# Two small rows, D and the shift weights, moved from ScalarE's DMA queue to the head of SyncE's

## The chip, the cores and the metric

The kernel runs on one NeuronCore of a Trainium2 chip. The metric is the device time of one execution in microseconds; a median of several runs is given with its lowest and highest. The engines are TensorE (PE, with its weight loads as PEld), VectorE (DVE), ScalarE (ACT), GpSimd (POOL) and SyncE (SP). SyncE and ScalarE can issue DMA transfers; the issuing instructions stand in the profile as SPq and ACTq.

## The reference

Two independent parts are computed, and their outputs stand side by side in one array of 2048 x 1152 in bf16. All inputs are bf16; S is 2048 and D is 576.

Part A is a long convolution per channel. With `kv = (k shifted and weighted by 4 taps) * v`:

```
k_shift = sum over t of k_pad[:, t:t + S, :] * shift_k[:, 3 - t]
kv      = k_shift * v
y       = irfft(rfft(kv padded to 2S) * rfft(ssm_k padded to 2S))[:S]   # along S, per channel
out_A   = q * (y + kv * ssm_D)
```

Part B is linear attention with 32 heads of 18 channels:

```
q, k, v = split(x @ wqkv);  phi(t) = where(t > 0, t + 1, exp(t)) + 1e-6
kv = einsum(phi(k), v);  z = sum over s of phi(k)
out_B = (einsum(phi(q), kv) / (einsum(phi(q), z) + 1e-6)) @ wo
```

## The kernel before

Part A is a transform of length 4096 made of matmuls. The 576 channels are cut into five chunks (`ACH`: four of 128, one of 64). A chunk of the filter (`h_sb`) is loaded with channels on partitions, transposed on TensorE into `hT`, and goes through a first stage (`h1`: matmuls with the matrices `G`, evicted into `Ch`), a transpose by DMA (`ht`, from `Ch` to `Cth`) and a second stage (`h2`). The signal kv goes the same way (`u1`, `ut`, `u2`). Products of the two, an inverse in two stages (`i1`, `i2`) and the multiplication by q follow. The term `kv * ssm_D` costs no pass of its own: D is added to the filter's first tap. The matrices `G` are made on the chip: VectorE computes indices (`ix`, tiles `mp` and `mc`), and ScalarE takes sines of them (`sin`). The second stage's small matrices come from GpSimd's indices (`iv`) and another sine (`sw`), after which ScalarE changes its table to the exponential.

Part B loads x in four groups of 512 rows (`x_sb`), transposes them on TensorE into `xT` (`x_D`; evicted by VectorE for groups 2 and 0), multiplies by the weights `wqk` for k and q, forms phi with an exponential on ScalarE and a multiply-max on VectorE, and then the head sums and the output matmuls.

The order of the work is written out by hand. `ORDER` is a string of some 300 units such as `ls` or `hT.0.D/21`; each unit's name stands for a function, the parts after dots are its arguments, and the digits after the slash choose buffers (PSUM places and rings). Every engine and every queue executes its share of the units in this order, and a waiting instruction holds up what stands behind it on its engine.

The head of the order, before: `io` (index rows by GpSimd, and the first sine on ScalarE, which loads its table); `ls` (load_shift, line 371: VectorE sets ones, ScalarE's queue loads the 4608-byte row of shift weights to one partition); `wu.0` (VectorE zeroes an operand); `ix.0.0`; `wu.1.A` (warm-up: five matmuls of zeros, line 81); `dl` (load_D, line 416: two memsets by VectorE, then ScalarE's queue loads the 1152-byte row of D); `id`, `iw` (identity and small indices); `sin.1.0`; `dc` (turn_D, line 422: five matmuls of one column turn the row of D into a column, which ScalarE copies to `Dcol`); `ix.0.1`; then the first chunks on SyncE's queue, `hl.0` (filter chunk 0), `xl.2` (x group 2), `hl.1` (filter chunk 1); `hd.0` (h_D, line 492: ScalarE adds D to the first tap of chunk 0); `Wj.A` (shift_w, line 376: matmuls with a column of ones spread the shift row to 128 partitions, ScalarE evicts them in three pieces); `hT.0.D` (line 498: 16 transposes of chunk 0, VectorE evicts); `sin.1.1`; `xl.0`; `xd.2` (16 and 4 transposes of x group 2, VectorE evicts both); `hd.1`; `sin.0.0` and `sin.0.1`; `hT.1`; and the first stages `h1`.

On SyncE's queue, the transfers follow one another so: filter chunk 0, x group 2, filter chunk 1, x group 0, three pieces of `wqk` with three pieces of k between the second and the third, and then the first transpose `ht.0.0`.

```
zero = K.sm[:, 1984:2048].bitcast(BF)
...
for _ in range({'A': 5, 'B': 8, 'C': 11, 'D': 14}[n]):
    nc.tensor.matmul(ps[:], lhsT=zero, rhs=zero.unsqueeze(1).to_broadcast([128, 4, 128]), start=True, stop=True)
```

Of the kernel before, what the change touches and what calls it, by code (L numbers as in the profile page):

```python
# [17 lines left out]
D = 576  # L18
# [11 lines left out]


ORDER = """
io ls wu.0 ix.0.0/0 wu.1.A/0 dl id iw sin.1.0 dc/1 ix.0.1 hl.0/0 xl.2 hl.1/1 ix.1.0/1 hd.0 ix.1.1 Wj.A/230 hT.0.D/21
sin.1.1 xl.0 xd.2.DD/023 hd.1 sin.0.0 sin.0.1 lw.2 hT.1.D/00 h1.0.0.1.A/01 h1.0.0.0.D/2 lw.1 h1.0.1.0.A/3 wm kl.0
h1.0.1.1.A/0 h1.1.1.0.A/11 iv lw.0 sw wk xd.0.DD/123 k.10/0 k.8/1 k.11/2 W k.2/3 ht.0.0/0 h1.1.0.0.A/0 cv.0.0.D k.0/1
k.1/2 hc h1.1.0.1.A/3 cv.0.1.DP k.3/0 q.2.1/1 k.9/2 h1.1.1.1.A/3 vl.0/0 cv.0.2.DD qt.0/0 xl.3 h2.0.0.1.A/01
# [37 lines left out]
def _warm(tc, psum, K, n):  # L74

    nc = tc.nc
    zero = K.sm[:, 1984:2048].bitcast(BF)
    if n:
        ps = psum.tile([128, 4, 128], FP32, name="warm_ps")
        for _ in range({'A': 5, 'B': 8, 'C': 11, 'D': 14}[n]):  # L80
            nc.tensor.matmul(ps[:], lhsT=zero, rhs=zero.unsqueeze(1).to_broadcast([128, 4, 128]), start=True, stop=True)
    else:
        nc.vector.memset(zero, 0.0)
# [162 lines left out]
def kernel(  # L246
# [13 lines left out]
    nc = tc.nc  # L260
# [87 lines left out]
    K = Consts()  # L348
# [17 lines left out]
    Wj = lpool.tile([128, 4, D], BF, name="Wj")  # L366
# [4 lines left out]
    def load_shift():  # L371
        K.Srow = pqT[0:1].rearrange("o c n -> o (c n)")[:, 0:4 * D]
        nc.vector.memset(K.sm[0:1, 769:833].bitcast(BF), 1.0)
        nc.scalar.dma_start(out=K.Srow, in_=A_shift_k.rearrange("(o d) j -> o (d j)", o=1))

    def shift_w(eng='A'):
        one = K.sm[0:1, 769:833].bitcast(BF)
# [38 lines left out]
    def load_D():  # L416
        K.Drow = K.sm[0:1, 448:769].bitcast(BF)
        nc.vector.memset(K.Drow[:, 576:640], 0.0)
        nc.vector.memset(K.Drow[:, 640:641], 1.0)
        nc.scalar.dma_start(out=K.Drow[:, 0:576], in_=A_ssm_D.rearrange("(o d) -> o d", o=1))  # L420

    def turn_D():
        K.D = ab.tile([128, 5], FP32, name="Dcol")
# [189 lines left out]
    B = {}  # L613
# [195 lines left out]
    def store_A(i):  # L809
# [5 lines left out]

    UNITS = {
        'xl': load_x, 'wm': one_w, 'lw': load_w, 'ls': load_shift, 'Wj': shift_w, 'eps': eps_col,
        'dl': load_D, 'dc': turn_D, 'id': lambda: _ident(tc, cpool, K), 'io': lambda: _small(tc, cpool, slotx, K),
        'ix': lambda p, h: _dft_index(tc, slotx, K, p, h), 'iv': lambda: _w16_phase(tc, K),
        'iw': lambda: _w16_index(tc, K), 'wk': lambda: _w16_mask(tc, K), 'sin': lambda ri, h: _sine(tc, cpool, K, ri, h),  # L820
# [17 lines left out]
        'i1': i1, 'i2': i2, 'st': store_A,  # L838
        'k': b_k, 'q': b_q, 'qt': b_qt, 'lwv': load_wv, 'wom': wo_M, 'lwo': load_wo, 'G': b_G, 'zs': b_z, 'kv': b_kv, 'M': b_M,
        'den': b_den, 'wu': lambda *n: _warm(tc, psum, K, n[-1]), 'bc': b_bc, 'bt': b_bt, 'o': b_out, 'ol': b_last,  # L840
    }
    with tc.manual_schedule():
        for unit in ORDER.split():
            unit, _, places = unit.partition("/")
# [33 lines left out]
```

## Time and profile before

| | |
|---|---|
| median of 3 runs (lowest to highest) | 164.46 us (163.96 to 164.61) |
| the profiled execution's own time | 162.77 us |
| its span, first to last instruction | 161.0 us |
| TensorE matmuls busy | 148.7 us (92%) |
| VectorE busy | 139.0 us (86%) |
| ScalarE busy | 127.3 us (79%) |
| GpSimd busy | 66.2 us (41%) |
| SyncE's DMA queue, packets' time | 89.2% of 16 engines' span |
| ScalarE's DMA queue | 4 packets, 0.01 MB |
| granted TensorE clock, mean | 0.999 |

Times in the profile are microseconds from the first instruction. A row of the timeline has the start, the duration, the engine, the line of the kernel, the operation, the tile written and the tiles read, and in brackets the engine's idle time before it with what ended that. Matmuls are pipelined and their ends are modelled. The chain of waits goes back from the last instruction to what released it, step by step, and is printed in order of time; a row has start, duration and name. A list of waits names the waiting instruction, what it waited for, the total, how often and the longest. The table of stretches gives for each stretch its length and, for each engine, busy time and number of instructions, then the granted clock, the share of the DMA engines' time and the GB/s. A DMA row's last number is the time from issue to landing.

### The profile page before, as it was taken

Reading aid. Unit: us, or ns where it says so; the run is one execution under the profiler, and the core shown is the slowest. Engines: PE = TensorE matmul, PEld = TensorE weight load, DVE = VectorE, ACT = ScalarE, POOL = GpSimd, SP = SyncE. Lnnn points to the kernel's source line nnn. Section 1 sums busy time; section 2 is a strip of 40 time slices with the busy share of each in tenths; the row PEclk is TensorE's granted clock in tenths of the full one; section 3 lists DMA queues with packets and bytes.
Section 4 is the critical chain, followed back from the end, with each engine's and each line's share of the span. In section 5 each row is a group of like instructions: output and inputs, shape, how many; then the busy total and the mean of one; then the engine's idle time right before and its main releaser. Section 6 shows DMA issues by size and latency. Waiting matters only on the chain.

```text
span 161.0 us, 4590 instructions
## 1 busy us (share of the span) xinstructions
PE 148.7 (92%) x1980; PEld 92.6 (58%) x1998; DVE 139.0 (86%) x171; ACT 127.3 (79%) x154; POOL 66.2 (41%) x68
## 2 busy tenths in 40 slices
PE   5699999999999999999999996999888999999982
PEld 1298555555643466657557476587545566578641
DVE  7969499699999898997999997998999989899631
ACT  5598786997998999998999674899987957596312
POOL 3007741806511819109000049199999068320000
PEclk9999999999999999999999999999999999999999
DMA  4999999592939699979999996698599995435175
GB/s 150 390 276 291 204 264 275 167 156 105 175 85 196 179 141 308 220 149 316 177 219 262 229 198 143 120 216 193 157 241 181 317 210 130 122 93 150 44 220 195
DMA packets 73084, 31.65 MB, mean 197 GB/s; under 512 B 50988, under 2 KB 72423, under 8 KB 73064
## 3 DMA queue, kind: packets, MB, share of 16 engines
q1 hardware_dynamic: 73060, 31.35, 89.2%
q8 instruction: 15, 0.25, 0.6%
q14 instruction: 5, 0.04, 0.1%
q10 hardware_dynamic: 4, 0.01, 0.0%
HBM read 14.97 MB, written 4.72 MB: 122 GB/s over the span
## 4 chain that ended last, share of the span: by engine, by line
PE 59%; DVE 14%; ACT 11%; DMA 7%; POOL 2%; issue 2%; SPq 1%; DVEq 0%; ACTq 0%
PE q_ps L456 11%; PE k_ps L447 9%; PE o_ps L773 8%; PE s_ps L551 5%; PE s_ps L528 5%; DMA wv_GT<-in_B_wqkv_dram 5%; PE i_ps L585 4%; DVE pqT L743 4%; ACT Cu L301 3%; ACT V L301 3%; PE g_ps L656 2%; DMA sm<-in_A_ssm_D_dram 2%; DVE at L486 2%; PE i_ps L598 2%; PE hT_ps L507 2%
## 5 line engine op out<-in xcount | busy, mean ns | idle before, releaser
L447 PE MATMUL k_ps<-wqk,xT 128*128 128x512 bf16 (+1 forms) x154 | 21.4, 282 | 0.4
L301 ACT ACTIVATE Ch<-s_ps 128x1024 bf16<-128x1024 f32 (+1 forms) x18 | 16.4, 953 | 3.9 <-PE s_ps L528 3.8
L528 PEld LDWEIGHTS <-G 128*128 128x128 bf16 x320 | 17.6, 98 | 3.0 <-issue 1.9
L456 PE MATMUL q_ps<-xT,wqk 128*128 128x512 bf16 x77 | 18.3, 379 | 0.2
L301 ACT ACTIVATE V<-i_ps 128x1024 bf16<-128x1024 f32 x17 | 16.6, 1039 | 1.3 <-PE i_ps L585 1.0
L447 PEld LDWEIGHTS <-xT 128*128 128x128 bf16 x160 | 11.4, 98 | 10.9 <-issue 0.9
L656 PE MATMUL g_ps<-pk,x_sb 128*128 128x65 bf16 (+1 forms) x124 | 16.3, 283 | 0.2
L301 ACT ACTIVATE T<-s_ps 128x1024 bf16<-128x1024 f32 x16 | 15.7, 1022 | 0.8 <-PE s_ps L551 0.8
L301 ACT ACTIVATE ob<-o_ps 128x576 bf16<-128x576 f32 (+1 forms) x11 | 6.8, 630 | 11.7 <-PE o_ps L765 7.8
L301 ACT ACTIVATE Cu<-s_ps 128x1024 bf16<-128x1024 f32 (+1 forms) x17 | 15.9, 984 | 0.0
L486 DVE TENSOR_TENSOR at<-at 128x2048 bf16<-128x2048 bf16 (+1 forms) x13 | 14.9, 1143 | 0.5
L485 DVE TENSOR_TENSOR at<-k,Wj 128x2048 bf16<-128x2048 bf16 (+1 forms) x13 | 14.8, 1136 | 0.4 <-POOL at L486 0.4
L301 ACT ACTIVATE SU<-s_ps 128x1024 bf16<-128x1024 f32 x14 | 14.1, 1044 | 0.6 <-PE s_ps L551 0.6
L773 PE MATMUL o_ps<-wo_M,pqT 128*128 128x64 bf16 (+1 forms) x107 | 14.1, 282 | 0.5 <-issue 0.3
L563 POOL TENSOR_TENSOR X<-SU,T 128x2048 bf16<-128x2048 bf16 x3 | 12.4, 4130 | 4.1 <-DMA Cth<-Ch 4.1
L483 POOL TENSOR_TENSOR at<-k,Wj 128x2048 bf16<-128x2048 bf16 (+1 forms) x2 | 6.2, 3094 | 19.1 <-PE s_ps L551 18.5
L440 DVE SCALAR_TENSOR_TENSOR pk<-pk,k_ps 128x576 bf16<-128x576 bf16 x16 | 11.8, 750 | 2.4 <-ACT pk L439 2.4
L656 PEld LDWEIGHTS <-x_sb 128*128 128x128 bf16 x128 | 8.5, 97 | 8.5 <-issue 0.8
L439 ACT ACTIVATE pk<-k_ps,neg 128x576 bf16<-128x576 f32 x16 | 11.6, 743 | 1.4 <-PE k_ps L447 1.0
L456 PEld LDWEIGHTS <-wqk 128*128 128x128 bf16 x80 | 7.4, 98 | 8.7 <-issue 0.9
L600 DVE TENSOR_TENSOR q<-i_ps,q 128x1024 bf16<-128x1024 f32 (+1 forms) x10 | 11.0, 1113 | 0.9 <-PE i_ps L599 0.9
L773 PEld LDWEIGHTS <-pqT 128*128 128x128 bf16 x112 | 7.5, 98 | 7.3 <-issue 0.7
(160 smaller groups left out, 346.2 us busy)
## 6 DMA issues: line engine op xcount, KB each, us to landing
x_sb<-in_B_x_dram SPq DMA_DIRECT2D x4, 576.0 KB, 6.4
h_sb<-in_A_ssm_k_dram SPq DMA_DIRECT2D x4, 512.0 KB, 4.3
out_dram<-ob SPq DMA_DIRECT2D x7, 288.0 KB, 2.7
k<-in_A_k_dram SPq DMA_DIRECT2D x1, 1280.0 KB
v<-in_A_v_dram SPq DMA_DIRECT2D x1, 1280.0 KB
q<-in_A_q_dram SPq DMA_DIRECT2D x1, 1280.0 KB, 8.7
wqk<-in_B_wqkv_dram SPq DMA_DIRECT2D x2, 576.0 KB
k<-in_A_k_dram SPq DMA_DIRECT2D x1, 1024.0 KB
```

The source lines that it names most:

```text
L301: nc.scalar.activation(out=out, in_=in_, func=ACT.Copy)
L439: nc.scalar.activation(out=out_ap, in_=ps_ap, func=ACT.Exp, bias=K.neg1[0:n, :])
L440: nc.vector.scalar_tensor_tensor(out=out_ap, in0=out_ap, scalar=1.0, in1=ps_ap, op0=ALU.min, op1=ALU.max)
L447: nc.tensor.matmul(ps[:, n0:n1], lhsT=xT[r // 4][:, t, rr * 128:(rr + 1) * 128], rhs=wqk[:, t, D + n0:D + n1], start=(t == 0), stop=(t == 4))
L456: nc.tensor.matmul(ps[:, j, :], lhsT=wqk[:, t, 128 * c:128 * c + 128], rhs=xT[g][:, t, :], start=(t == 0), stop=(t == 4))
L485: on[0].tensor_tensor(out=t_, in0=kk[:, 3 - stage:19 - stage], in1=wb(stage), op=ALU.mult)
L486: on[1].tensor_tensor(out=a_, in0=a_, in1=t_, op=ALU.add)
L528: nc.tensor.matmul(ps[:, bi, 0:dc], lhsT=K.G[ri][:, b, :], rhs=xf(b), start=True, stop=True)
L563: e.tensor_tensor(out=s['X', hf][:], in0=s['SU', hf][:], in1=t[:, :, ::-1, :], op=ALU.mult)
L600: nc.vector.tensor_tensor(out=qs, in0=ps[:, :, 0:dc], in1=qs, op=ALU.mult)
L656: nc.tensor.matmul(ps[:, n0:n1], lhsT=x_sb[:, r, f0:f0 + fn], rhs=pk[:, r, n0:n1], start=(r == 0), stop=(r == 15))
L773: nc.tensor.matmul(pss[i][:, n0:n1], lhsT=pqT[:, c, r * 128:(r + 1) * 128], rhs=B['M'][:, c, n0:n1], start=(c == 0 and not first), stop=(c ...
```

## The change

Four places are edited. `dl` moves in the order from behind the warm-up to the second place, ahead of `ls`. Both rows are issued by SyncE instead of ScalarE. So SyncE's queue begins with D, then the shift weights, then filter chunk 0 and the rest as before; VectorE's two memsets of `dl` come ahead of those of `ls` and `wu.0`. The number of warm-up matmuls for the letter D in the table is changed, too.

```diff
 ORDER = """
-io ls wu.0 ix.0.0/0 wu.1.A/0 dl id iw sin.1.0 dc/1 ix.0.1 hl.0/0 xl.2 hl.1/1 ix.1.0/1 hd.0 ix.1.1 Wj.A/230 hT.0.D/21
+io dl ls wu.0 ix.0.0/0 wu.1.A/0 id iw sin.1.0 dc/1 ix.0.1 hl.0/0 xl.2 hl.1/1 ix.1.0/1 hd.0 ix.1.1 Wj.A/230 hT.0.D/21
...
-        for _ in range({'A': 5, 'B': 8, 'C': 11, 'D': 14}[n]):
+        for _ in range({'A': 5, 'B': 8, 'C': 11, 'D': 1}[n]):
...
     def load_shift():
...
-        nc.scalar.dma_start(out=K.Srow, in_=A_shift_k.rearrange("(o d) j -> o (d j)", o=1))
+        nc.sync.dma_start(out=K.Srow, in_=A_shift_k.rearrange("(o d) j -> o (d j)", o=1))
...
     def load_D():
...
-        nc.scalar.dma_start(out=K.Drow[:, 0:576], in_=A_ssm_D.rearrange("(o d) -> o d", o=1))
+        nc.sync.dma_start(out=K.Drow[:, 0:576], in_=A_ssm_D.rearrange("(o d) -> o d", o=1))
```

## The prediction

> **What bounds the kernel now.** I read the page's first line, then the list of TensorE's waits over the whole span, then the chain of waits from its start, and then the first 17 us engine by engine.
>
> ```profile
> span 161.0 us, 4590 instructions
> ```
>
> The profiled execution took 162.77 us, 1.8 us more than its span, and lies 1.69 us under the median of the runs shown, 164.46. I work on this execution's time axis and carry the difference in microseconds over to the median.
>
> TensorE's waits (instruction <- what it waited for: total, times, longest):
>
> ```profile
> PE D_ps L426 <- DMA sm<-in_A_ssm_D_dram: 1.8, 1, 1.8
> PE kv_ps L681 <- DMA wv_GT<-in_B_wqkv_dram: 1.4, 1, 1.4
> PE warm_ps L81 <- DVE sm L83: 1.3, 1, 1.3
> PE o_ps L790 <- ACT ob L301: 0.5, 1, 0.5
> ```
>
> TensorE is never kept waiting long once it is going: one wait of 1.4 us, one of 0.5, the rest shorter. The longest is at the head, and it is the one that the change is about: five 1-column matmuls that turn the row of D wait for its transfer. The chain of waits starts there:
>
> ```profile
> 1.49 3.85 DMA sm<-in_A_ssm_D_dram
> 5.39 0.28 PE D_ps L426 x5
> ...
> 12.50 0.51 POOL xT L346
> ```
>
> From D's landing at 1.49 + 3.85 = 5.34 us the chain goes on without a break through TensorE, VectorE's eviction of xT and GpSimd's memset behind it. So time won at 5.34 can reach the end, as long as nothing else has become late by then.
>
> Why the row came so late is seen in the queues (start, duration of the issue):
>
> ```profile
> 0.80 0.39 SPq L434 DMA_DIRECT2D h_sb<-in_A_ssm_k_dram  x1
> 1.25 0.42 SPq L321 DMA_DIRECT2D x_sb<-in_B_x_dram  x1
> ```
>
> and in the time from issue to landing of these two, the last number of each row:
>
> ```profile
> h_sb<-in_A_ssm_k_dram SPq DMA_DIRECT2D x1, 512.0 KB, 3.9
> ```
>
> ```profile
> x_sb<-in_B_x_dram SPq DMA_DIRECT2D x1, 576.0 KB, 5.1
> ```
>
> The filter chunk lands at 4.70, the x chunk at 6.35, and D, issued between them in time, at 5.34: the order of landing is nearly the order of issue, whichever queue issued it. The stretches of the head (last three columns: granted clock, DMA share, GB/s) say the same:
>
> ```profile
> 1.00:3.00 2.00, 1.73 (x5) 0.57 (x5) 1.90 (x4) 1.29 (x2) 1.22 (x13) 1.00 0.38 109
> 3.00:17.00 14.00, 11.87 (x130) 9.04 (x130) 11.05 (x22) 10.90 (x14) 3.96 (x12) 1.00 1.10 323
> ```
>
> Up to 3 us the DMA engines are mostly idle, after that they are full until 17 us. A row issued first meets empty engines.
>
> The engines' own order in the head, ScalarE with its queue, TensorE, VectorE (what stands in brackets is the idle time before):
>
> ```profile
> 0.97 0.49 ACTq L374 DMA_DIRECT2D pqT<-in_A_shift_k_dram  x1
> 1.49 0.21 ACTq L420 DMA_DIRECT2D sm<-in_A_ssm_D_dram  x1
> ...
> 3.27 1.15 ACT L224 ACTIVATE G<-mp,negpi 128x1024 bf16<-128x1024 int32 x1 [0.97 <-DVE sm L419]
> 5.71 0.18 ACT L428 ACTIVATE Dcol<-D_ps 128x5 f32<-128x5 f32 x1 [1.30 <-PE D_ps L426]
> 5.92 0.30 ACT L496 ACTIVATE h_sb<-h_sb,Dcol 128x1 bf16<-128x1 bf16 x1
> 6.59 2.22 ACT L301 ACTIVATE Wj<-W_ps 128x1024 bf16<-128x1024 f32 x3 [0.37 <-PE W_ps L383]
> ...
> 9.71 0.30 ACT L496 ACTIVATE h_sb<-h_sb,Dcol 128x1 bf16<-128x1 bf16 x1
> 9.90 2.19 ACT L224 ACTIVATE G<-mc,negpi 128x1024 bf16<-128x1024 int16 x2
> 12.63 3.77 ACT L301 ACTIVATE Ch<-s_ps 128x1024 bf16<-128x1024 f32 x4 [0.53 <-PE s_ps L528]
> ```
>
> ```profile
> 1.27 2.31 PE L81 MATMUL warm_ps<-sm 128*128 128x512 bf16 x5 [1.27 <-DVE sm L83]
> ...
> 5.54 2.08 PE L383 MATMUL W_ps<-pqT,sm 1*128 1x512 bf16 x5
> 7.55 1.92 PE L507 MATMUL hT_ps<-ident,h_sb 128*128 128x128 bf16 x16
> 9.27 1.58 PE L339 MATMUL xT_ps<-ident,x_sb 128*128 128x128 bf16 x16
> ...
> 10.90 1.18 PE L507 MATMUL hT_ps<-ident,h_sb 128*128 128x128 bf16 x16
> ```
>
> ```profile
> 3.17 0.09 DVE L418 MEMSET sm<- 1x32 uint32 x1
> ...
> 7.53 0.43 DVE L153 TENSOR_SCALAR mc<-mc 128x1024 int16<-128x1024 int16 x1
> 9.51 1.22 DVE L303 COPY hT<-hT_ps 128x2048 bf16<-128x2048 bf16 x1 [1.55 <-PE hT_ps L507]
> 10.88 1.56 DVE L303 COPY xT<-xT_ps 128x2048 bf16<-128x2048 bf16 x2
> ```
>
> **The change, part by part.** Edits with one answer first. The warm-up table's entry for the letter D is not reached: the order names only A. The two issues leave ScalarE's queue; ScalarE's first sine waits for VectorE at 3.27 anyway, with 0.97 us idle before it, so nothing is won there. Two memsets of one partition move ahead of the warm-up's operand on VectorE, at 0.09 us or less each: the warm-up and the index work start up to 0.18 us later, I take 0.10, and VectorE has it back at 3.17, where they are gone. The warm-up then ends at 1.27 + 2.31 + 0.10 = 3.68.
>
> SyncE's queue issues two more transfers ahead of all its chunks. On ScalarE's queue the two took from 0.97 to 1.49 + 0.21 = 1.70, 0.73 us; no row shows them on SyncE's. The lower end is nothing (the engines begin slowly anyway), the upper twice that, 1.5. I take 0.73, the row of the same two transfers. The first filter chunk then lands at 4.70 + 0.73 = 5.43, the x chunk at 7.08; behind them are moved the second filter chunk, the other x chunk, the weights and k.
>
> D's landing: at best it takes its issue, 0.21, and at worst the 3.85 us that it took before, so between 1.0 and 4.65. Everything up to 3.68 is hidden behind the warm-up, that is, up to 2.9 us. I take it as hidden, since the row meets empty engines. The shift row, issued next, is needed only behind D's matmuls, at 3.83.
>
> TensorE: D's matmuls at 3.68 instead of 5.39, 1.71 us earlier. The shift weights' matmuls run 3.83 to 5.91, and the first filter transposes can start at 7.55 - 1.71 = 5.84. They need the filter chunk with D added: landing 5.43, addition on ScalarE 0.30, so 5.76. It fits with 0.08 us over. Here the chunk takes the place of D as what comes last; each further 0.1 us of its delay costs 0.1.
>
> VectorE is next: its index work is dense until 7.53 + 0.43 = 7.96 and does not move. The filter's 16 transposes end at 5.84 + 1.92 = 7.76, so the eviction of hT starts at 7.96 instead of 9.51, 1.55 us earlier, and ends at 9.18. The x transposes start at 9.27 - 1.71 = 7.56, after the chunk's 7.08, and take 1.92 at the speed of the first filter transposes: 9.48. So the eviction of xT starts between 9.18 and 9.5 instead of at 10.88: 1.4 to 1.7 us earlier.
>
> The same 16 transposes take 1.92 us at 7.55 and 1.18 at 10.90, while the granted clock reads 1.00 throughout: TensorE gets faster on the way, within 5.5 us of the start of D's matmuls at 5.39, from where it is busy without a break. [...]
>
> ScalarE: the additions at 5.46 to 5.76, then the shift weights' evictions at once, 0.83 earlier than 6.59. From there it is dense to 9.90 + 2.19 = 12.09, so its sines end at 11.26 and the first eviction of Ch starts there instead of at 12.63: 1.37 us earlier. The second filter chunk, 524 kB at 323 GB/s or 1.6 us behind the x chunk, lands near 8.7 (an estimate from these rows); ScalarE adds D to it at 9.71 - 0.83 = 8.88. That also fits.
>
> The sum is thus 1.37 (ScalarE) to 1.7 us (VectorE): I take 1.4, the smaller, since the evictions of Ch feed the rest. The x matmuls, the index work on GpSimd and the exponentials follow in order and are all moved by it. The DMA engines are the one thing that is not earlier but 0.7 later, and what they have in hand is seen where the queue first stands still for an engine again:
>
> ```profile
> SPq L535 <- PE s_ps L551: 3.8, 1, 3.8
> ```
>
> SyncE waits 3.8 us there for TensorE (within the first 30 us), against 1.4 + 0.7 = 2.1 that are used up. So 162.77 becomes 161.4, and the median 164.46 becomes 163.1, 0.85% less.
>
> **The rivals.** One: the row's 3.85 us are its own and travel with it. D lands at 0.80 + 3.85 = 4.65, the matmuls start at 4.70 instead of 5.39, 0.69 us are won: 163.8. For it: the row is a single tiny transfer, and no row shows one on idle engines. Against it: its landing lies in issue order between two chunks. [...] The landings (4.70, 5.34, 6.35) speak rather for one line of all. 0.11.
>
> Two: the start is won and lost again at a transfer. The place is the head's loads or the 1.4 us wait of kv_ps, whose load is the second DMA on TensorE's path; if the DMA engines, full from 3 to 17 us, hold the later work to their own time, the end is where it was: 164.4. Against it: the 3.8 us above. 0.09.
>
> Three, slower: the rows hold up SyncE's queue by more than their issue, and the filter chunk becomes the late one. The addition to the chunk stands before the shift weights' evictions on ScalarE; it begins to cost against now when the chunk lands after 6.29 (1.6 us later than 4.70), and TensorE when it lands after 7.25. If the queue were to begin its chunks only when D's row, at 3.85 us, is done, the chunk would land at 0.80 + 3.85 + 3.9 = 8.55, the transposes start at 8.9 instead of 7.55, and the end is 1.35 later: 165.8. Against it: the x chunk lands 1.65 us behind the filter chunk though it takes 5.1, so transfers of one queue overlap. 0.08.
>
> **How the numbers follow.** The forecast has 0.72: its own range is 162.7 to 163.6 (1.0 to 1.75 us won). Half a per cent, 0.82 us, is about what a measurement of this kernel can tell from no change; the runs of before alone spread by 0.65. Faster by more than that is the forecast, 0.72; within it are rivals one and two, 0.20; slower is rival three, 0.08. The range goes from 162.4 (1.7 won and 0.3 of spread) up to 164.3, which takes in rival one and most of two, and leaves out three.
>
> **What would show it.** Right: D's row on SyncE's queue at 0.80, landing before 3.7; no wait on D in TensorE's list; D's matmuls at 3.7; ScalarE's addition waiting for the filter chunk to about 5.4; the eviction of hT close behind 7.96, that of xT near 9.3, the first of Ch near 11.3, and the same lead at 20 and 30 us. Wrong: D landing after 4 us (rival one); the lead there at 12 us and gone at 30 or at kv_ps (two); the filter chunk after 6.3 us (three). [...]

## The result, and the profile after

| | before | after |
|---|---|---|
| median of 4 runs each, on one chip (lowest to highest) | 164.25 us (163.96 to 164.61) | 161.61 us (161.44 to 162.44) |
| profiled execution's own time | 162.77 us | 162.44 us |
| its span | 161.0 us | 160.7 us |

The ratio is 0.9848 (95% interval 0.9807 to 0.9889): 2.64 us or 1.5% faster. The sign was forecast, but the size was not: 163.1 us would be 0.9915 (1.4 of 164.46 less), outside the interval, and 161.61 lies below the whole range. (The 164.25 has a fourth run beside the three that were known.) Executions far above the fastest of their kernel, such as the 164.27 us of e6 (mean granted clock 0.977) and the 165.04 of e9 (0.989), are left out of the ratios; medians and spreads keep them. The two profiled executions, on the other hand, lie only 0.33 us apart. That of before is faster than any of its four timed runs, that of after is the slowest of its four. This contradiction is the subject of most of what follows.

The head of the profile of after, engine by engine. First SyncE's queue (start, duration of the issue), and the row of the first filter chunk in the table of transfers, whose last number is the time from issue to landing:

```profile
0.80 0.35 SPq L420 DMA_DIRECT2D sm<-in_A_ssm_D_dram  x1
1.21 0.23 SPq L374 DMA_DIRECT2D pqT<-in_A_shift_k_dram  x1
1.48 0.37 SPq L434 DMA_DIRECT2D h_sb<-in_A_ssm_k_dram  x1
```

```profile
h_sb<-in_A_ssm_k_dram SPq DMA_DIRECT2D x1, 512.0 KB, 3.6
```

The two rows push the filter chunk's issue from 0.80 to 1.48, yet it lands at 1.48 + 3.6 = 5.08, only 0.38 us later than the 4.70 of before. The timelines of TensorE, ScalarE and VectorE:

```profile
1.33 2.32 PE L81 MATMUL warm_ps<-sm 128*128 128x512 bf16 x5 [1.33 <-DVE sm L83]
3.58 0.29 PE L426 MATMUL D_ps<-sm 1*128 1x1 bf16 x5
3.73 2.08 PE L383 MATMUL W_ps<-pqT,sm 1*128 1x512 bf16 x5
5.74 1.93 PE L507 MATMUL hT_ps<-ident,h_sb 128*128 128x128 bf16 x16
7.46 1.91 PE L339 MATMUL xT_ps<-ident,x_sb 128*128 128x128 bf16 x16
...
14.49 5.10 PE L447 MATMUL k_ps<-wqk,xT 128*128 128x512 bf16 x39
```

```profile
4.32 0.16 ACT L428 ACTIVATE Dcol<-D_ps 128x5 f32<-128x5 f32 x1
5.14 0.30 ACT L496 ACTIVATE h_sb<-h_sb,Dcol 128x1 bf16<-128x1 bf16 x1 [0.66 <-DMA h_sb<-in_A_ssm_k_dram]
5.34 2.19 ACT L301 ACTIVATE Wj<-W_ps 128x1024 bf16<-128x1024 f32 x3
...
11.42 1.94 ACT L301 ACTIVATE Ch<-s_ps 128x1024 bf16<-128x1024 f32 x2 [0.59 <-PE s_ps L528]
...
90.37 1.93 ACT L301 ACTIVATE T<-s_ps 128x1024 bf16<-128x1024 f32 x2
...
157.62 0.41 ACT L301 ACTIVATE ob<-o_ps 128x288 bf16<-128x288 f32 x1 [0.33 <-PE o_ps L796]
```

```profile
7.83 1.22 DVE L303 COPY hT<-hT_ps 128x2048 bf16<-128x2048 bf16 x1
9.41 1.56 DVE L303 COPY xT<-xT_ps 128x2048 bf16<-128x2048 bf16 x2 [0.36 <-PE xT_ps L339]
...
96.48 2.76 DVE L565 TENSOR_TENSOR T<-SU,T 128x2048 bf16<-128x2048 bf16 x1
```

D's matmuls no longer wait: they follow the warm-up at 3.58. What comes last now is the filter chunk, for which ScalarE's addition waits to 5.14. The matmuls for k (L447), a good mark for the end of the head, begin at 14.49. In the profile of before, as later in the same view and in the same order, the rows are

```profile
15.87 3.40 PE L447 MATMUL k_ps<-wqk,xT 128*128 128x512 bf16 x22
```

```profile
91.84 1.93 ACT L301 ACTIVATE T<-s_ps 128x1024 bf16<-128x1024 f32 x2
...
157.88 0.41 ACT L301 ACTIVATE ob<-o_ps 128x288 bf16<-128x288 f32 x1 [0.33 <-PE o_ps L796]
```

So the lead is 1.38 us at the marks for k, 1.47 at ScalarE's T, at 90 to 92 us, and 0.26 at the last eviction. It is there for more than half of the kernel and is lost in this pair between 92 and 103 us. The place shows in VectorE's product L565 above, which takes 2.76 us in the profile of after, where GpSimd's sum L568, on the other half of the products, started ahead of it:

```profile
96.03 2.12 POOL L568 TENSOR_TENSOR X<-X 128x1024 bf16<-128x1024 bf16 x1
```

In the profile of before VectorE came first, and the prices are the other way round:

```profile
97.13 1.22 DVE L565 TENSOR_TENSOR T<-SU,T 128x2048 bf16<-128x2048 bf16 x1
```

```profile
97.49 2.84 POOL L568 TENSOR_TENSOR X<-X 128x1024 bf16<-128x1024 bf16 x1
```

In these two profiles, whichever starts second takes longer, VectorE by 1.5 us (2.76 against 1.22) and GpSimd by 0.7 (2.84 against 2.12). What the order costs is seen in the chain of waits. In the profile of before it runs through the load of `wv_GT` and TensorE's `kv_ps`, and VectorE's product is not on it:

```profile
99.11 1.46 PE kv_ps L681 x25
100.66 0.99 DVE wo_M L684 x5
```

In the profile of after it runs through the long product:

```profile
96.56 2.67 DVE T L565
...
100.29 0.98 DVE wo_M L684 x5
```

At `kv_ps` the lead is still 1.38 us (97.73 against 99.11), at VectorE's next step L684 it is 0.37. So in this pair GpSimd first costs 1.0 us on the path, and VectorE first does not.

### The profile page after: what moved, and what is told of

It reads as the page before. It is cut to its first block, busy times and chain, and to the rows that moved or that the text cites. A ratio compares the mean times of both kernels' runs of the same rounds, so it can differ in the third digit from the quotient of the medians.

```text
span 160.7 us, 4590 instructions
## 1 busy us (share of the span) xinstructions
PE 149.4 (93%) x1980; PEld 93.6 (58%) x1998; DVE 140.6 (87%) x171; ACT 127.2 (79%) x154; POOL 65.4 (41%) x68
## 4 chain that ended last, share of the span: by engine, by line
PE 69%; ACT 11%; DMA 7%; DVE 5%; issue 3%; POOL 2%; ACTq 0%; DVEq 0%
PE q_ps L456 11%; PE k_ps L447 9%; PE o_ps L773 8%; PE g_ps L656 6%; PE s_ps L551 6%; PE s_ps L528 5%; PE i_ps L585 4%; DMA Cth<-Ch 4%; ACT Cu L301 3%; DMA Ctu<-Cu 3%; ACT V L301 3%; PE hT_ps L507 2%; PE i_ps L598 2%; ACT T L301 2%; PE i_ps L599 2%
## 5 line engine op out<-in xcount | busy, mean ns | idle before, releaser
L447 PE MATMUL k_ps<-wqk,xT 128*128 128x512 bf16 (+1 forms) x154 | 21.3, 282 | 0.4
L447 PEld LDWEIGHTS <-xT 128*128 128x128 bf16 x160 | 11.3, 98 | 10.8 <-issue 0.9
L528 PE MATMUL s_ps<-v,G 128*128 128x128 bf16 (+1 forms) x160 | 11.0, 214 | 1.0 <-ACT Cu L301 0.9
```

What stands on the lines that cost most here:

```text
L447: nc.tensor.matmul(ps[:, n0:n1], lhsT=xT[r // 4][:, t, rr * 128:(rr + 1) * 128], rhs=wqk[:, t, D + n0:D + n1], start=(t == 0), stop=(t == 4))
L528: nc.tensor.matmul(ps[:, bi, 0:dc], lhsT=K.G[ri][:, b, :], rhs=xf(b), start=True, stop=True)
```

## The experiments

My first theory was that the profiled execution of before was untypical, and its rival that the change wins more somewhere behind the head than I had seen. Another question ran beside these: why D's row was late at all, and whether TensorE's rate in the head belongs to the sum: in the profile of before 16 transposes take 1.92 us at 7.55 (the slow rate) and 1.05 at 14.75 (the fast rate). Every measured ratio is against the kernel before on the same chip.

**The kernel before once more**, no edit.

> The kernel before, unchanged, as a control. The head's lead of the changed kernel in the two profiles is 1.47 us up to 84 us, but its median is 2.6 us lower. Theory A (the head is all, the rest is chance in the middle): before's own execution on record (162.77) was a good one; another one of it loses time between 85 and 100 us, where TensorE waits for the load of wv_GT or for transposes, so its span lies 1 to 2 us above 161.0 and the extra stands after 85 us. Theory B (the clock at the head): the extra time stands before 20 us, because TensorE's fast rate begins later than 10.3 us in most executions of before. Ratio 1.00 in both.

Measured: 164.41 us (163.35 to 164.88, 12 runs), ratio 0.9987 (0.9955 to 1.0018). Its profiled execution took 164.73, 2 us more than the one I had read. Its TensorE, VectorE and GpSimd:

```profile
5.70 0.29 PE L426 MATMUL D_ps<-sm 1*128 1x1 bf16 x5 [2.12 <-DMA sm<-in_A_ssm_D_dram]
...
9.59 1.91 PE L339 MATMUL xT_ps<-ident,x_sb 128*128 128x128 bf16 x16
...
16.68 3.69 PE L447 MATMUL k_ps<-wqk,xT 128*128 128x512 bf16 x25
```

```profile
98.57 2.79 DVE L565 TENSOR_TENSOR T<-SU,T 128x2048 bf16<-128x2048 bf16 x1
```

```profile
98.15 2.12 POOL L568 TENSOR_TENSOR X<-X 128x1024 bf16<-128x1024 bf16 x1
```

D lands 0.3 us later, the x transposes take 1.91 instead of 1.58, and the matmuls for k start at 16.68 instead of 15.87. At 98 us GpSimd is first, as in the profile of after. So the record of before had been a good one twice, in the head (theory B) and behind 97 us (theory A): each theory holds for a part of the 2 us.

**The kernel after once more**, no edit.

> The changed kernel, unchanged, as a control and for a narrower interval. Theory A: a ratio of 0.985 to 0.991 (1.5 to 2.5 us), D landing near 2.1 us, the lead over before 1.4 to 1.5 us at 20 us and at 80 us, and a time after 85 us that differs from profile to profile. Theory B: the lead at 20 us differs from profile to profile by 0.5 us or more.

Measured: 162.16 us (161.29 to 162.77, 6 runs), ratio 0.9863 (0.9819 to 0.9907). The head repeats the profile of after: the matmuls for k start at 14.38, and GpSimd is first at 96.06. Against the second profile of before the lead is 2.30 us at the matmuls for k and 1.89 at the last eviction: with the same order at 97 us on both sides, most of it reaches the end. A third profile of the kernel before (e11):

> The kernel before, unchanged, one more profile, on another day of the same kind. If the execution on record was an unusually good one: D lands at 5.5 to 5.8, the fast rate begins after 11 us, the x matmuls for k start after 16.3 (15.87 on record) and the span is 162 to 163.5. If not: 5.3 to 5.4, 10.4, 15.9 and 161.

```profile
5.22 0.29 PE L426 MATMUL D_ps<-sm 1*128 1x1 bf16 x5 [1.64 <-DMA sm<-in_A_ssm_D_dram]
...
15.94 3.41 PE L447 MATMUL k_ps<-wqk,xT 128*128 128x512 bf16 x23
```

This one took 164.1 us: D at 5.22, k at 15.94, and GpSimd first. A late D spreads from 5.22 to 5.70. The head does not follow from it alone: in the first profile D comes at 5.39 and k sooner than here, at 15.87, since the x transposes took 1.58 there and 1.81 here.

**D alone at the head of SyncE's queue.** The shift row stays with ScalarE:

```diff
 # against the kernel after, in load_shift
-        nc.sync.dma_start(out=K.Srow, in_=...)
+        nc.scalar.dma_start(out=K.Srow, in_=...)
```

> Only D is moved to the head of SyncE's queue; the shift row stays on ScalarE's queue. Theory A (the whole head's win is D's landing): D lands near 2.1 us, the filter chunk about 0.3 us earlier than in the changed kernel's 5.05 since one issue less stands before it, the shift row lands before 3.8; the lead is 1.4 to 1.6 us at 20 us and the time within 0.3% of the changed kernel. Rival (the shift row must go too): the shift row lands after 4 us, its matmuls wait, and half the lead or more is gone.

Measured: 162.26 us, ratio 0.9876 (0.9831 to 0.992). The filter chunk is added to at 4.83 instead of 5.14, but the matmuls for k start at 14.39, as in the two profiles of the kernel after (14.49, 14.38). So the 0.3 us that the second row costs SyncE's queue (the chunk is issued at 1.21 instead of 1.48) are not on the path, and moving one row gives the same within the interval.

**D first, but both rows on ScalarE's queue.** Only the order changes:

```diff
-io ls wu.0 ix.0.0/0 wu.1.A/0 dl id iw ...
+io dl ls wu.0 ix.0.0/0 wu.1.A/0 id iw ...
```

> D is issued first, as in the change, but both rows stay on ScalarE's queue, so SyncE's chunks are issued as in the kernel before (0.80). Theory A (only the place in the order of issue counts, not the queue): D, issued at 1.0 between the filter chunk and the x chunk, lands with the filter chunk near 4.7 or before it, D's matmuls run at 4.8 at the latest, and a third to all of the lead is kept. Rival (the queue counts): D lands as late as 5.3 whatever its place on ScalarE's queue, and nothing is won. If D lands under 3.6 us, this version is as good as the changed one or 0.3 us better, since the chunks aren't pushed back.

Measured: 164.04 us, ratio 0.9985 (0.9959 to 1.0011). TensorE and ScalarE:

```profile
3.68 0.29 PE L426 MATMUL D_ps<-sm 1*128 1x1 bf16 x5
5.26 2.07 PE L383 MATMUL W_ps<-pqT,sm 1*128 1x512 bf16 x5 [1.29 <-DMA pqT<-in_A_shift_k_dram]
```

```profile
4.68 0.30 ACT L496 ACTIVATE h_sb<-h_sb,Dcol 128x1 bf16<-128x1 bf16 x1 [0.20 <-DMA h_sb<-in_A_ssm_k_dram]
```

D is in time, although it is issued at 0.97, behind the filter chunk's 0.80, and the chunk is waited for until 4.68: the landing does not follow the order of issue. Now the shift row, issued second on ScalarE's queue at 1.51, is the late one: it lands 3.7 us after its issue, and TensorE waits 1.29 us for it. The wait has only changed its owner.

**The shift row alone on SyncE's queue**, D staying where it was, as the only transfer of ScalarE's:

```diff
 # against the kernel before, in load_shift
-        nc.scalar.dma_start(out=K.Srow, in_=...)
+        nc.sync.dma_start(out=K.Srow, in_=...)
```

> The kernel before with one edit: the shift row goes to the head of SyncE's queue, D stays on ScalarE's queue, where it is now the first and only row. Theory C (the first row on ScalarE's queue lands soon, the second is late): D, issued at about 1.0, lands before 3.7, TensorE doesn't wait for it, and the time falls by 1.8 to 2.4 us, as in the changed kernel. Rival (D must be ahead of the filter chunk): D lands after 4.5 us, and less than 1 us is won.

Measured: 162.26 us (161.58 to 163.18, 6 runs), ratio 0.9885 (0.9842 to 0.9928). SyncE's and ScalarE's queues and TensorE:

```profile
1.21 0.38 SPq L434 DMA_DIRECT2D h_sb<-in_A_ssm_k_dram  x1
```

```profile
0.97 0.50 ACTq L420 DMA_DIRECT2D sm<-in_A_ssm_D_dram  x1
```

```profile
3.52 0.29 PE L426 MATMUL D_ps<-sm 1*128 1x1 bf16 x5
```

D is issued by ScalarE, ahead of the filter chunk in time, and is not waited for. So D need not stand on SyncE's queue: the second row of ScalarE's queue was late, whichever it was (D 3.85 us from issue to landing in the profile of before, the shift row 3.70 in e4), and either may leave (theory C). One rival is not separated from this: in every profile with a late row it was issued at 1.49 to 1.51, behind two of SyncE's loads, and every row that came in time was issued by 1.21 with at most one large load ahead of it. Being second is not enough by itself, since SyncE's second row, the shift weights issued at 1.21, is there by 2.62 in e7 below. Moving the shift row, whose issue took 0.49 us in the profile of before, was worth about 1.9 us (0.0115 x 164.14, the median of before beside it), more than its issuing time.

**A small load between the filter chunk and x.** If the second row stands behind the bytes of SyncE's first loads, a small second load should help: the 144 kB piece `lw.2` of the weights comes ahead of x group 2.

```diff
-... hl.0/0 xl.2 hl.1/1 ...
+... hl.0/0 lw.2 xl.2 hl.1/1 ...
```

> The kernel before with the small piece of wqk (144 KB) moved up to the second place of SyncE's queue, ahead of the x chunk (576 KB), so that D on ScalarE's queue is issued behind 656 KB instead of 1088 KB. Theory F (one line in the order of issue over both queues): D lands 0.5 to 1.2 us earlier than the 5.3 to 5.7 of the kernel before, behind the small piece. Rival (D's time is its own, 3.9 to 4.2 us from its issue on this queue): D lands at 5.3 or later all the same.

Measured: one time, 164.65 us. D is issued at 1.51, and its matmuls start at 5.22, to the hundredth where the unchanged kernel of e11 has them. Theory F is not borne out, though a few tenths would be lost in the spread of D's landing. Why the row is late stays open.

**No warm-up in the kernel after.** The five warm-up matmuls of zeros, which feed nothing, are left out:

```diff
-        for _ in range({'A': 5, 'B': 8, 'C': 11, 'D': 1}[n]):
+        for _ in range({'A': 0, 'B': 8, 'C': 11, 'D': 1}[n]):
```

> The changed kernel without the five warm-up matmuls (they feed nothing). D's matmuls then start when D lands, 2.1 us, the shift matmuls at 2.7, and the first filter transposes when the filter chunk has landed and been added to, near 5.4 instead of 5.74. Theory E (behind D the filter chunk, and then VectorE at 7.9, set the pace): 0.1 to 0.35 us are won at the eviction of xT. Rival (the warm-up is needed for the fast rate): it begins 0.5 us or more later than 9.7, and the time grows by 0.2 to 0.8 us.

Measured: 162.37 us (161.03 to 163.09), ratio 0.9879 (0.9833 to 0.9925). TensorE:

```profile
2.12 0.29 PE L426 MATMUL D_ps<-sm 1*128 1x1 bf16 x5 [2.12 <-DMA sm<-in_A_ssm_D_dram]
2.62 2.08 PE L383 MATMUL W_ps<-pqT,sm 1*128 1x512 bf16 x5 [0.21 <-DMA pqT<-in_A_shift_k_dram]
5.41 1.92 PE L507 MATMUL hT_ps<-ident,h_sb 128*128 128x128 bf16 x16 [0.71 <-ACT h_sb L496]
7.13 1.91 PE L339 MATMUL xT_ps<-ident,x_sb 128*128 128x128 bf16 x16
```

With its cover gone, D's landing can be read: about 2.1, 1.3 us after its issue at 0.80, against 3.85 before. The filter chunk shows as the next bound (5.41). And the first transposes take 1.92 and 1.91 us, as with five warm-ups (1.93 and 1.91), so five do nothing for these.

**Nine warm-ups in the kernel before** ('A': 9 instead of 5), D as late as ever.

> The kernel before with nine warm-up matmuls instead of five, so that TensorE's wait for D is filled with work on zeros up to about 5.3 us; everything else stays. Theory D (the closed gap brings TensorE's fast rate forward): the fast rate begins before 9.5 us instead of 10.4 to 12.2, the x transposes take under 1.6 us, and 0.3 to 0.6 us are won although D lands no sooner. Rival (the fast rate begins some 4 us after the first full transposes, whatever the warm-up): it begins 3.9 to 4.4 us after the first filter transposes, and the time is within 0.2% of the kernel before.

Measured: 162.33 us (160.89 to 164.27, 6 runs), ratio 0.9894 (0.9836 to 0.9951). The profiled execution is the fastest of the six, 160.89:

```profile
1.27 3.84 PE L81 MATMUL warm_ps<-sm 128*128 128x512 bf16 x9 [1.27 <-DVE sm L83]
5.39 0.27 PE L426 MATMUL D_ps<-sm 1*128 1x1 bf16 x5 [0.28 <-DMA sm<-in_A_ssm_D_dram]
5.53 1.13 PE L383 MATMUL W_ps<-pqT,sm 1*128 1x512 bf16 x5
6.59 1.22 PE L507 MATMUL hT_ps<-ident,h_sb 128*128 128x128 bf16 x16
7.64 1.06 PE L339 MATMUL xT_ps<-ident,x_sb 128*128 128x128 bf16 x16
```

In this execution TensorE had the fast rate by the time D came, behind 3.84 us of full-tile matmuls (W_ps 1.13 instead of 2.08, the x transposes 1.06 instead of 1.91), and the matmuls for k start at 14.48, as early as with the change: theory D, in this execution. Without the two longest, too, the runs go from 160.89 to 162.4, and one execution alone was profiled, so how often this works is not shown.

**Nine and twelve warm-ups in the kernel after.**

> The changed kernel with nine warm-up matmuls instead of five. Theory G (the fast rate begins when TensorE has worked on full tiles for long enough, and the matmuls on one partition don't count): it begins near 5 us in executions where the moment falls well, the shift matmuls take 1.1 instead of 2.1 us, the x transposes 1.1 instead of 1.9, the eviction of xT starts at 9.05 instead of 9.41, and the lead over the changed kernel is 0.3 to 0.5 us; where it falls badly, D's matmuls are 1.5 us later than in the changed kernel and up to 1 us is lost, so the runs spread over 1.5 us or more. Rival (TensorE's rate doesn't matter behind VectorE's 7.9): within 0.2% of the changed kernel, in all runs.

> The changed kernel with twelve warm-up matmuls. Theory G: enough work on full tiles for the fast rate to begin in nearly every execution before D's matmuls, between 4.7 and 6.5 us; once it has begun, a warm-up takes half as long. Then a median 0.2 to 0.6 us under the changed kernel's and a smaller spread than with nine. Rival: the warm-ups beyond five only stand in the way, D's matmuls start at 6.5, and 0.7 to 1.3 us are lost.

Nine: 161.9 us (160.39 to 165.04, 11 runs), ratio 0.9843 (0.981 to 0.9876). Twelve: 161.74 (160.74 to 164.05, 6 runs), ratio 0.9822 (0.9779 to 0.9865). Both overlap with the plain kernel after (0.9848, 0.9863). The profile of nine is of its slowest execution, and there the rate behind the same nine matmuls was still the slow one (W_ps 2.08, the first 16 transposes 1.92), at a granted clock that reads 1.00 up to 80 us:

```profile
1.33 4.02 PE L81 MATMUL warm_ps<-sm 128*128 128x512 bf16 x9 [1.33 <-DVE sm L83]
...
7.44 1.92 PE L507 MATMUL hT_ps<-ident,h_sb 128*128 128x128 bf16 x16
```

With twelve (4.39 us) the fast rate came in the one execution profiled (W_ps 1.13), yet the matmuls for k start at 14.76 there, later than the 14.49 and 14.38 of the plain kernel after: the longer warm-up costs what the rate wins. On the median neither number wins.

**x before the filter chunk**, to price the new bound:

```diff
-... hl.0/0 xl.2 hl.1/1 ...
+... xl.2 hl.0/0 hl.1/1 ...
```

> The changed kernel with the x chunk ahead of the first filter chunk on SyncE's queue, so that the filter chunk lands about 1.6 us later than 5.05. Theory A (the filter chunk has taken D's place as what comes last, with some 0.4 us to spare): the addition of D runs near 6.7, the first filter transposes start near 7.0 instead of 5.74, and 0.9 to 1.3 us of the lead are gone at 20 us. Rival (VectorE's 7.9 and later work cover the chunk): under 0.4 us are lost.

Measured: 163.67 us (162.38 to 164.2, 10 runs), ratio 0.9959 (0.9928 to 0.999). ScalarE and TensorE:

```profile
6.90 0.30 ACT L496 ACTIVATE h_sb<-h_sb,Dcol 128x1 bf16<-128x1 bf16 x1 [2.42 <-DMA h_sb<-in_A_ssm_k_dram]
```

```profile
7.25 1.93 PE L507 MATMUL hT_ps<-ident,h_sb 128*128 128x128 bf16 x16 [1.45 <-ACT h_sb L496]
```

An addition 1.76 us later starts the transposes 1.51 later and the matmuls for k at 16.09: most of the gain is gone. The filter chunk is what the head waits for next, with some 0.3 us of slack (in the profile of after the addition to it ends at 5.44 and the transposes start at 5.74).

**The interference at 97 us taken out on both sides.** GpSimd's sum L568 (the unit `pA.1.0`, its last part naming the engine) goes to VectorE, so that no order of the two is left. (The expectation counts GpSimd first in eight of thirteen profiles; by the traces it is nine of the fourteen up to e12.)

```diff
-... h1.3.0.0.A/1 pA.1.0.P pS.1.0.D
+... h1.3.0.0.A/1 pA.1.0.D pS.1.0.D
```

> The kernel before, with one sum of X (line 568, GpSimd near 97 us) on VectorE instead. In eight of thirteen profiles so far it starts just ahead of VectorE's product into T (line 565), which then takes 2.8 to 3.1 us instead of 1.22, and about 1 us of the lead is lost. Theory H (the time differs between executions by which of the two starts first, and the kernel before mostly has the slow order): the product takes 1.22 us, and 0.5 to 1.0 us are won against the kernel before. Rival (the place is covered by the wait for wv_GT's load): within 0.3 us of the kernel before.

> The changed kernel with the same sum of X on VectorE. Theory H, with the changed kernel mostly in the fast order outside of its profiles: 0 to 0.4 us are won against the changed kernel, and the distance to the kernel before with the same edit is the head's lead alone, 1.5 to 2.1 us instead of 2.3 to 2.6. Rival (the order at 97 us has no part in the distance): both win the same, and the distance stays 2.3 to 2.6 us.

The kernel before with this edit: 163.1 us (162.41 to 163.64, 12 runs), ratio 0.9941 (0.9914 to 0.9967). The kernel after with it: 161.28 us (160.97 to 161.63, 6 runs), ratio 0.9839 (0.9807 to 0.9871). VectorE's product is short in both:

```profile
97.89 1.22 DVE L565 TENSOR_TENSOR T<-SU,T 128x2048 bf16<-128x2048 bf16 x1
```

```profile
96.55 1.22 DVE L565 TENSOR_TENSOR T<-SU,T 128x2048 bf16<-128x2048 bf16 x1
```

The edit takes 163.96 - 163.1 = 0.9 us off the kernel before, by the medians beside each other, and by the ratios to the kernel before (0.9839 against 0.9848 and 0.9863) 0.1 to 0.4 off the kernel after, which was not run beside it. The distance of the two is 163.1 - 161.28 = 1.82 us, instead of 2.64. In the two profiles the matmuls for k start at 16.08 and 14.33, 1.75 us apart, and the last eviction is 1.94 apart. The last experiment adds the twelve warm-ups to the edited kernel after:

> The changed kernel with twelve warm-up matmuls and the sum of X on VectorE, both edits together, as a candidate for the fastest version. If each is worth what the runs before suggest (0 to 0.4 us each), the median is 161.2 to 161.8 and the ratio to the kernel before 0.980 to 0.984. If the two don't add, it is that of the changed kernel, 0.985 to 0.987.

Measured: 161.59 us (160.74 to 162.75), ratio 0.9859 (0.9817 to 0.9902). The two do not add: the fast rate comes (W_ps 1.13), but the matmuls for k start at 15.00 instead of 14.33. The kernel after with the sum on VectorE has the smallest spread of all versions with six or more runs, 0.66 us, and no version was measurably faster.

## Why the prediction was right about the way and wrong about the size

**D is hidden, rival one is refuted.** Forecast: matmuls at 3.68, landing somewhere between 1.0 and 4.65, taken as before 3.68. They start at 3.58, and without the warm-up D is there at about 2.1. The row's 3.85 us were not its own (some 1.3 us from issue to landing in e7).

**The reason for the late row was not borne out.** It was that "the order of landing is nearly the order of issue, whichever queue issued it". In e4 D is issued behind the filter chunk and is there about a microsecond ahead of it (3.68 against 4.68). e5 does not test this, since D's issue at 0.97 stands ahead of the chunk's 1.21 there. What the late rows have in common is the second place on ScalarE's queue and an issue at 1.49 to 1.51; which of the two decides is open.

**The issues cost SyncE what was said, and the chunk less.** 0.73 us forecast, 1.48 - 0.80 = 0.68 measured; the chunk lands at 5.08 instead of 5.43. It takes the place of D as what comes last, as forecast, with a slack of some 0.3 us instead of 0.08. Rival three would have needed 6.29.

**The chain through the engines held.** First transposes 5.84 forecast, 5.74 measured; eviction of hT 7.96 and 7.83; of xT 9.18 to 9.5 and 9.41; first Ch 11.26 and 11.42. SyncE's wait for TensorE within the first 30 us fell by 1.5 us, where 2.1 were reckoned with:

```profile
SPq L535 <- PE s_ps L551: 2.3, 1, 2.3
```

Rival two has the lead used up by the transfers, in the head or at `kv_ps`. The lead of 1.4 us is there, 1.38 us at the matmuls for k, 1.47 at T and 1.38 at `kv_ps`; where this pair loses it afterwards, VectorE and GpSimd do it, and between the second profiles of the two kernels most of it reaches the end (1.89 of 2.30).

**TensorE's rate.** The sum stood between 1.4 (ScalarE) and 1.7 (VectorE's 9.18, which asks for x transposes of some 1.6 us from 7.56, where 1.92 was taken). The transposes took 1.93 and 1.91, and the eviction of xT starts at 9.41, so the value taken was right. TensorE is busy from 1.33 on without a pause, and yet 16 transposes take 1.91 us at 7.46, then 1.28 at 9.59 and 1.05 at 13.38. Whether the closed gap brings the fast rate forward is not shown: with D early the x transposes took 1.91 (after, e2, e3, e7), 1.85 (e14) and 1.62 (e5), with D late 1.58 to 1.91 (before, e1, e8, e11, e13).

**What failed** is the step ahead of the sum: "I work on this execution's time axis and carry the difference in microseconds over to the median." It failed in two places. First, the term of 1.4 for the head was too small. The starting points of the sum (D's matmuls at 5.39, xT evicted at 10.88, Ch at 12.63) came from one execution, and it was a good one. The matmuls for k start at 15.87 in it, but at 16.68, 15.94 and 16.08 in the three other profiles with the head unchanged (e1, e11, e13): 16.14 on the average of four. With the head changed they start at 14.49, 14.38 and 14.33 (after, e2, e14), 14.40 on average. So the head is worth 1.74 us on average, and between 1.38 and 2.35 by pairs; the term of 1.4 was the low end of this. The 1.69 us between the profile and the median was written down and then treated as if it lay outside of the stretch that the change touches. Second, what follows the head was taken to be "all moved by it", so the rest of the kernel was put at nothing. The head's 1.74 alone would give 164.46 - 1.74 = 162.7 us, inside the range of the forecast; the result lies outside because of the rest.

**The rest, some 0.9 us of the 2.64,** is explained in part. The one place that the runs show is the one at 97 us. In the nine profiles up to e12 with GpSimd first, VectorE's L684 starts 9.91 to 9.93 us after ScalarE's T; in the five with VectorE first it is 8.40 to 9.35, and with the sum on VectorE (e13 to e15) 8.74 to 9.14. In all nine TensorE waits 0.2 to 0.6 us for ScalarE's `Cu` some 4 us ahead of T, and none of the five shows that wait; e13 and e14 have this wait as well (0.3 and 0.7) and still reach L684 early, so it goes with the order but does not cost the time. e13 and e14 stand 1.82 us apart, near the head's share. This fits a kernel before that has GpSimd first in most of its timed runs and a kernel after that has it less often. But only profiled executions show the order, and the two of the kernel after both have GpSimd first; it is inferred from the times, since three of its four runs lie below its profiled one. The rival is the draw of a few runs: e2, e3, e5 and e7, in which D is as early, are 1.9 to 2.3 us faster than before (ratios 0.9863 to 0.9885), and all these intervals overlap with that of the 2.64. So this part is supported and not settled.

## What to carry to other kernels

One profile is one execution: if it lies outside the timed runs, the difference is somewhere, and a second profile of the same kernel tells whether it lies in the stretch that a change touches, before any term is taken from it. When a tiny transfer is late, ask what else is on its queue: here either of two rows could leave, and changing their order only passed the wait on. When instructions of two engines overlap and their times change from profile to profile (VectorE's product here 1.22 or 2.76 us), see who starts first in each profile before reading a difference behind that point as an effect of the change.

## What the runs showed of the hardware beyond what was expected

- A row of a few kB issued second on ScalarE's queue, at 1.49 to 1.51, landed 3.7 to 4.2 us after its issue (D 3.85 in the profile of before and 4.16 in e1, the shift row 3.70 in e4); as the first of SyncE's, it landed after some 1.3 us (e7), as the second of SyncE's within 1.4 us (issued at 1.21, matmuls at 2.62 in e7), and as the only one of ScalarE's within 2.6 us (issued at 0.97, not waited for at 3.52 in e5).
- TensorE's rate in the head does not follow from busy time alone: behind 2.3 us of warm-up and 2.4 us of one-partition matmuls the first 16 transposes took 1.93 us in both profiles of the kernel after; behind nine full-tile matmuls W_ps and these transposes took 1.13 and 1.22 in e6 (the nine 3.84 us) and 2.08 and 1.92 in e9 (4.02 us), behind twelve 1.13 and 1.21 in e10 (4.39 us) and 1.13 and 1.22 in e15 (4.65 us). Whether the one-partition matmuls count was not tried by itself.
- VectorE's product of two tiles takes 1.22 us alone or ahead of GpSimd's sum, and 2.75 to 3.15 when it starts behind it; GpSimd's sum takes 2.12 to 2.14 ahead and 2.77 to 2.84 behind. When VectorE is second, its product ends 1.08 to 1.09 us after GpSimd's sum in all nine profiles (99.24 and 98.15 in that of after), that is, nearly the 1.22 us that it takes alone. Which of them is first changes between executions of one kernel (before: VectorE in one profile, GpSimd in two).
